# Queueing the preparation of a head pair six steps earlier, with the hi/lo split kept at its place

## The chip, the core and the metric

One core of a Trainium2 chip runs the whole program. The time is the device time of one execution in microseconds (us); the figures shown are medians over several executions. A profile is one execution taken apart by the hardware profiler.

## What is computed

Attention with a cluster mask, then a dense two-layer MLP, then a routed one (8 experts). The part that matters here is the attention, over batch 2, 8 heads, 768 positions and 64 channels:

```python
q_assign = np.argmax(np.einsum('bhsd,hcd->bhsc', q_n, c_n), axis=-1)
k_assign = np.argmax(np.einsum('bhsd,hcd->bhsc', k_n, c_n), axis=-1)
mask = q_assign[:, :, :, None] == k_assign[:, :, None, :]
scores = scale * np.matmul(q, k.transpose(0, 1, 3, 2))
scores = np.where(mask, scores, -1000000000.0)
...
attn = np.exp(scores)
attn = attn / (np.sum(attn, axis=-1, keepdims=True) + 1e-09)
return np.matmul(attn, v).astype(np.float32)
...
h = x @ w_in
g = np.maximum(0.01 * h, h)
return (g @ w_out).astype(np.float32)
```

## The kernel before, in words

The 16 (batch, head) problems are taken as 8 pairs of heads. A pair is 12 steps, so the attention is 96 steps, and it fills about the first 300 us. A step s is one head's block of 128 query rows: four score matmuls into PSUM (L343: `sps<-UA/UB`, then `sps<-VA/VB`), the row maximum on DVE (L346), the exponential on ACT (L361), the transposes of the block of step s-3 (L400) and their evacuation on ACT (L407), and a share of the products with v (L415). Even steps are head 0 of the pair and read the tiles UA and VA, odd steps head 1 and read UB and VB. There are two PSUM buffers for scores, so PE can be one step ahead of ACT's exponential and no more.

**Preparation of a pair.** U and V hold q and k, each as a high and a low part, and in rows 64 to 79 of U the cluster mask. They are double buffered over pairs. They are made in a chain: load q and k (`natq`, `natk`, L99, on SP's queue); four groups of transposes on PE (`raw_pe`, L179, one per half of q and k); four copies to `raw` on ACT (`raw_act`, L186); a split of each into high and low on POOL (`raw_split`, L205 and L206); after the second half of q and of k, four copies each between the halves of U and V on SP's queue (L210 to L218, 64 x 768 float32 each; for k in the order `UB<-UA`, `VA<-VB`, `VB<-UA`, `VA<-UA`); beside it the cluster scores (`assign_pe`, `assign_act`), the argmax on DVE and POOL, the transposes of its result (`mask_pe`) and `mask_dve` (L289 and L294), which scales the mask on DVE and writes it into U by eight small copies on SP's queue, four into UA, then four into UB.

**What sets the order.** The step loop issues everything in program order, and each engine runs its instructions in that order. A table `PREP` says for each part of the chain in which step r it is issued, r counted from the start of the pair ahead (r = 0 of pair 2 is step 12). Before, the chain starts at r = -2 and its mask copies go out at r = 8. Pair 1 has a table of its own (`PREP1`), since its q and k are prepared ahead of the loop; pair 0 is prepared ahead of the loop altogether.

**Other traffic.** Every 5.5 steps `conv_step` stores one converted piece of the MLP's weights (L544, `w_f_scratch<-cvt`, 512 KB) and loads another (L519, `stg`, 1 MB), both on ACT's queue: at steps 10.5, 16, 21.5, 27, 32.5, 38, 43.5, 49, 54.5, 60, 65.5, 71, 76.5 and so on. Every six steps ACT's queue also gets the store of the reciprocals of the row sums (L652, at s = 6n + 3) and two loads that spread them over partitions (L386, `rb`, at s = 6n + 5); POOL then scales the output and splits it (`av_split`, L430 to L432).

**Semaphores of transfers.** In the built program the transfers that SP and ACT issue are given one of eight semaphores (DMAHW0 to DMAHW7) in rotation, and the instruction that issues a transfer first waits until the transfer that had its semaphore before has landed. It stands in its engine's order meanwhile. On ACT such a wait also holds the exponentials behind it, and two score buffers later it holds PE.

Of the kernel before, what the change touches and what calls it, by code (L numbers as in the profile page):

```python
# [20 lines left out]
def _f(ap):  # L21
    return ap.bitcast(F32)
# [3 lines left out]
def kernel(  # L26
# [66 lines left out]
    def load_qk(p):  # L93
        b, cc = divmod(p, NPAIR)
        for nm, src in (("q", q), ("k", k)):
            if p:
                t = att_a.tile([P, NT, 2, D], F32, tag="nat" + nm, name="nat" + nm)
                nat[nm, p] = t
                nc.sync.dma_start(t, src[b, 2 * cc:2 * cc + 2].rearrange("h (p t) d -> p t h d", t=NT))  # L99
            else:  # L100
                t = att.tile([P, 2, HS], F32R, tag="pr", name="first", bufs=4)
                t = _f(t.rearrange("p a b -> p (a b)")).rearrange("p (h t d) -> p h t d", h=2, d=D)
                nc.sync.dma_start(t, src[b, 0:2].rearrange("h (p t) d -> p h t d", t=NT))
                first[nm] = t
                nat[nm, 0] = nat0[:, "qk".index(nm)]
            if p == 0 and nm == "q":
                nc.sync.dma_start(cnat, centroids.rearrange("h c d -> (h c) d"))
# [59 lines left out]
    raw_t, uv_t, sc_t, oh_t = {}, {}, {}, {}  # L167
# [14 lines left out]
    def raw_act(p, i):  # L182
        qk, half = divmod(i, 2)
        ps = ps_prep.pop(("raw", i)).rearrange("p j c -> p (j c)")
        sc = SCALE if qk == 0 else 1.0
        nc.scalar.activation(out=raw_t[p][:, i, :], in_=ps, func=AF.Copy, scale=sc)  # L186
        if p:
            raw_split(p, i)

    def first_hi(i):  # L190
# [7 lines left out]
    def raw_split(p, i):  # L198
        raw = raw_t[p]
        UA, UB, VA, VB = uv_t[p]  # L200
        qk, half = divmod(i, 2)
        cs = slice(half * HS, (half + 1) * HS)
        hi = UA[:, qk, cs]
        lo = (VA if qk == 0 else VB)[:, qk, cs]
        nc.gpsimd.tensor_scalar(out=hi, in0=raw[:, i, :], scalar1=1.0, scalar2=1.0, op0=ALU.mult, op1=ALU.mult)  # L205
        nc.gpsimd.tensor_tensor(out=lo, in0=raw[:, i, :], in1=_f(hi), op=ALU.subtract)  # L206
        if half == 1:
            dma = nc.sync.dma_start
            U, W, X, Y = (_f(t[:, qk, :]) for t in (UA, UB, VA, VB))
            dma(W[0:64], U[64:128])  # L210
            if qk == 0:
                dma(Y[0:64], X[64:128])
                dma(Y[64:128], U[64:128])
                dma(X[64:128], U[0:64])
            else:
                dma(X[64:128], Y[0:64])
                dma(Y[0:64], U[64:128])
                dma(X[0:64], U[0:64])  # L218
# [67 lines left out]
    def mask_dve(p):  # L286
        UA, UB, VA, VB = uv_t[p]
        mk = att_a.tile([P, HS], F32R, tag="mk", name="mk")
        nc.vector.tensor_scalar(out=mk, in0=ps_prep["mk"].rearrange("p j c -> p (j c)"), scalar1=msc[:, 0:1],  # L289
                                scalar2=msc[:, 1:2], op0=ALU.mult, op1=ALU.add)  # L290
        for h, U in ((0, UA), (1, UB)):
            for i in range(4):
                qk, half = divmod(i, 2)
                nc.sync.dma_start(_f(U[64:80, qk, half * HS:(half + 1) * HS]),  # L294
                                  _f(mk[32 * i + 16 * h:32 * i + 16 * h + 16, :]))

    PREP = [
        (-2, "pb", raw_pe, 0), (-1, "a0", raw_act, 0), (-1, "pb", raw_pe, 1),
        (0, "a0", raw_act, 1), (0, "pb", raw_pe, 2), (1, "a0", raw_act, 2), (1, "pb", raw_pe, 3),
        (2, "a0", raw_act, 3), (2, "pb", assign_pe, None),  # L300
        (3, "a0", assign_act, None), (3, "pb", argmax_pe, None),
        (4, "d", argmax_0, None), (4, "d", argmax_1, None), (5, "d", argmax_2, None), (6, "d", argmax_3, None),
        (7, "pb", mask_pe, None), (8, "d", mask_dve, None),
    ]
    PREP1 = [(1, "pb", assign_pe, None), (2, "a0", assign_act, None), (2, "pb", argmax_pe, None), (3, "pb", argmax_0, None), (4, "pb", argmax_1, None), (5, "d", argmax_2, None), (6, "pb", argmax_3, None), (7, "pb", mask_pe, None), (8, "d", mask_dve, None)]

    def prep(p, r, slot):
        if p >= NP:
            return
        for rr, sl, f, arg in PREP1 if p == 1 else PREP:  # L310
            if rr == r and sl == slot:
                if f is raw_pe or f is raw_act:
                    f(p, arg)
                else:
                    f(p)
                if f is raw_act and arg == 3 and 1 < p < NP - 1:
                    load_qk(p + 1)
# [137 lines left out]
    UA, UB, VA, VB = uv_t[0]  # L455
# [27 lines left out]
    for r in range(3, 7):  # L483
        for slot in ("a0", "pa", "d", "pb"):
            prep(0, r, slot)
# [82 lines left out]

    def preps(p, r, slot):
        prep(p + 1, r, slot)  # L570
        if r >= 10:
            prep(p + 2, r - 12, slot)

    CONV0, CPER = 10, 11
# [62 lines left out]
    for s in range(NSTEP + 12 + LAG):  # L637
        p, r = divmod(s, 12)
        if s < NSTEP:
            st_scores(s)  # L640
        conv_step(s, 0)
        preps(p, r, "a0")
        preps(p, r, "pa")
        if 0 <= s - LAG < NSTEP:
            st_transpose(s - LAG)
# [17 lines left out]
        if 0 < gf <= NSTEP // 6 and rf < 2:  # L663
            recip(gf - 1, rf)
        preps(p, r, "d")
        preps(p, r, "pb")
        if r == 10 and p + 1 < NP:
# [703 lines left out]
```

## Time and profile before

| | before |
|---|---|
| runs | 712.04, 716.92, 717.11 us |
| median | 716.92 us |
| the profiled execution | 715.46 us, span 713.8 us |
| mean granted TensorE clock | 0.98 |
| PE busy | 657.3 us, 92% of the span |
| ACT, DVE, POOL busy | 424.6, 397.9, 261.1 us |

In the rows below, a timeline row gives start (us from the start of the span), duration in us, engine, line, operation, what it writes and reads, count, and in brackets how long the engine was idle ahead of it and what is taken to have released it. SPq and ACTq are the instructions with which SP and ACT issue transfers; their duration is that of the issue, not of the transfer.

### The profile page before, as it was taken

To read this page: it belongs to the slowest core of one execution; us is meant where nothing else is said; L and a number is where in the kernel's file an instruction comes from. 1 tells how busy PE (TensorE), PEld (TensorE's weight loads), DVE (VectorE), ACT (ScalarE), POOL (GpSimd) and SP (SyncE) were. 2 spreads that over 40 slices of the span, in tenths; PEclk is the share of its full clock that TensorE was granted. 3 is DMA by queue.
4 is the path that set the end of the run, shared out by engine and by line. 5 is a ranking of instruction groups with operands and counts; after the bars stand their busy time and mean duration, and the time that the engine had idled before them with its cause. 6 is when DMAs were issued, how large, how long until landed. Compare 5 with 4: busy or idle time off the path is not lost. (4 is left out here: it accounts for less than half of the span.)

```text
span 713.8 us, 10056 instructions
## 1 busy us (share of the span) xinstructions
PE 657.3 (92%) x3587; PEld 490.9 (69%) x3587; DVE 397.9 (56%) x687; ACT 424.6 (59%) x824; POOL 261.1 (37%) x263
## 2 busy tenths in 40 slices
PE   5869997989998999989999999999999989989995
PEld 3646664656665656568888888788888767767875
DVE  5747773767785667332222312543223637999993
ACT  5857875778787678644444444445444354757771
POOL 4222422425344211274456444444434356000412
PEclk9989998999999899999999999999999999999998
DMA  8776684666768554820000200003233147989970
GB/s 196 214 207 181 190 206 133 165 196 177 220 177 261 148 166 159 308 98 1 0 1 2 118 2 1 0 1 124 112 118 118 65 172 277 338 287 310 369 253 25
DMA packets 64723, 108.79 MB, mean 152 GB/s; under 512 B 27481, under 2 KB 33083, under 8 KB 63648
## 3 DMA queue, kind: packets, MB, share of 16 engines
q1 hardware_dynamic: 52944, 71.30, 32.8%
q10 hardware_dynamic: 9696, 30.46, 13.1%
q0 software_dynamic: 2032, 6.37, 2.6%
q8 instruction: 29, 0.48, 0.3%
q14 instruction: 22, 0.18, 0.1%
HBM read 77.71 MB, written 16.89 MB: 133 GB/s over the span
## 5 line engine op out<-in xcount | busy, mean ns | idle before, releaser
L346 DVE TENSOR_REDUCE st<-sps 128x1 f32<-128x768 f32 x96 | 91.6, 955 | 85.5 <-PE sps L343 85.0
L704 DVE TENSOR_TENSOR g<-ups,lk 128x512 f32<-128x512 f32 x48 | 33.2, 691 | 136.3 <-ACT lk L703 136.2
L407 ACT ACTIVATE pt<-tps 128x384 f32<-128x384 f32 x192 | 84.3, 495 | 36.0 <-PE tps L400 35.1
L361 ACT ACTIVATE pr<-sps,st 128x768 f32<-128x768 f32 x96 | 86.9, 906 | 22.4 <-DVE cvt L537 5.5
L607 POOL TENSOR_TENSOR wloi<-rawb,whii 128x512 fp32r<-128x512 f32 x36 | 46.6, 1294 | 105.5 <-ACT whii L605 105.5
L415 PE MATMUL avps<-pt,vnat 128*64 128x384 f32 x384 | 83.9, 521 | 0.0
L400 PE MATMUL tps<-ident,pr 128*128 128x128 f32 x576 | 81.4, 278 | 1.6 <-ACT pt L407 1.5
L400 PEld LDWEIGHTS tps<-ident,pr 128*128 128x128 f32 x576 | 69.8, 143 | 9.0 <-ACT pt L407 5.1
L631 PE MATMUL ups<-xh,wloi 128*128 128x512 f32 x192 | 74.8, 390 | 0.9 <-POOL wloi L607 0.9
L631 PE MATMUL ups<-xh,whii 128*128 128x512 f32 x192 | 74.8, 390 | 0.0
L631 PE MATMUL ups<-xl,whii 128*128 128x512 f32 x192 | 74.7, 389 | 0.0
L719 PE MATMUL acc<-wloo,gh 128*128 128x512 f32 x184 | 71.8, 390 | 2.0 <-POOL wloo L617 2.0
L719 PE MATMUL acc<-whio,gh 128*128 128x512 f32 x184 | 73.4, 399 | 0.0
L719 PE MATMUL acc<-whio,gl 128*128 128x512 f32 x184 | 71.8, 390 | 0.0
L703 ACT ACTIVATE lk<-ups 128x512 f32<-128x512 f32 x48 | 28.6, 595 | 65.6 <-PE ups L631 65.6
L430 POOL TENSOR_TENSOR xr<-xr,rb 128x384 f32<-128x384 f32 x16 | 16.4, 1023 | 103.0 <-ACT xr L423 86.5
L705 ACT ACTIVATE gh<-g 128x512 fp32r<-128x512 f32 x48 | 30.4, 632 | 38.3 <-DVE g L704 38.3
L706 DVE TENSOR_TENSOR gl<-g,gh 128x512 fp32r<-128x512 f32 x48 | 34.3, 715 | 33.5 <-ACT gh L705 33.5
L617 POOL TENSOR_TENSOR wloo<-rawb,whio 128x512 fp32r<-128x512 f32 x36 | 46.4, 1290 | 0.9 <-ACT whio L616 0.8
L343 PE MATMUL sps<-UB 80*128 80x384 f32 x96 | 30.6, 398 | 14.6 <-ACT pr L361 6.3
L932 DVE TENSOR_TENSOR xl<-rawb,xh 128x1024 fp32r<-128x1024 f32 x36 | 42.3, 1216 | 0.3 <-ACT xh L930 0.3
L631 PEld LDWEIGHTS ups<-xh,wloi 128*128 128x128 f32 x192 | 36.0, 188 | 8.8 <-POOL wloi L607 1.3
(291 smaller groups left out, 1341.7 us busy)
## 6 DMA issues: line engine op xcount, KB each, us to landing
rawb<-in_moe_w_dram SPq DMA_DIRECT2D x26, 1024.0 KB
stg<-in_moe_w_in_dram ACTq DMA_DIRECT2D x8, 1024.0 KB
w_f_scratch<-cvt ACTq DMA_DIRECT2D x16, 512.0 KB
stg<-in_moe_w_out_dram ACTq DMA_DIRECT2D x8, 1024.0 KB
rawa<-in_moe_w_dram SPq DMA_DIRECT2D x8, 1024.0 KB
rawb<-w_f_scratch SPq DMA_DIRECT2D x6, 1024.0 KB
vnat<-in_v_dram SPq DMA_DIRECT2D x8, 384.0 KB
rb<-recip_scratch ACTq DMA_DIRECT2D x32, 96.0 KB
```

The source lines that it names most:

```text
L346: nc.vector.tensor_reduce(out=st[:, 0:1], in_=ps[:, :, 0:HS], axis=AX.XY, op=ALU.max, negate=True)
L361: nc.scalar.activation(out=pr, in_=ps[:, :, 0:HS], func=AF.Exp, bias=st[:, 0:1], accum_out=sm_t[g][:, 3 * h + j:3 * h + j + 1])
L400: nc.tensor.transpose(ps[:, t, :], pr[:, kh, t * P:(t + 1) * P], ident)
L407: nc.scalar.activation(out=pt[:, 3 * kh:3 * kh + 3, j, :], in_=t_t[s][kh], func=AF.Copy)
L415: nc.tensor.matmul(av_t[g][64 * h:64 * h + 64, :], lhsT=vnat[p][:, h, kt, :], rhs=pt_t[p, half, h][:, kt].rearrange("p j c -> p (j c)"), s ...
L607: eng.tensor_tensor(out=lo, in0=src, in1=_f(hi), op=ALU.subtract)
L617: nc.gpsimd.tensor_tensor(out=lo, in0=src, in1=_f(hi), op=ALU.subtract)
L631: nc.tensor.matmul(ps, lhsT=w[:, cc, :], rhs=x[:, cc, cs], start=(n == 0), stop=(n == 3 * KD - 1))
L704: nc.vector.tensor_tensor(out=g, in0=ps, in1=t, op=ALU.max)
L706: nc.vector.tensor_tensor(out=gl, in0=g, in1=_f(gh), op=ALU.subtract)
L719: nc.tensor.matmul(ps, lhsT=a[:, ts_], rhs=w, start=(fc == 0 and n == 0), stop=(fc == NFC - 1 and n == 2))
L932: eng.tensor_tensor(out=lo, in0=src, in1=_f(hi), op=ALU.subtract)
```

## The change

The table becomes a function `plan(d)`: `PREP = plan(0)` starts the raw transposes at r = -8 and ends the mask on DVE at r = 2, six steps earlier than before. Pair 2 uses `plan(4)` (two steps earlier than before) and pair 3 `plan(2)` (four). `raw_split` no longer follows the raw copy at once: it has entries of its own at r = 0 to 3, one step later than before, and with it go its copies on SP's queue (r = 1 and 3 instead of 0 and 2). The eight mask copies become `mask_dma`, issued at r = 4 (pair 2: r = 6) instead of r = 8. The loads of the next pair's q and k, issued behind the last raw copy, move with it from r = 2 to r = -4. Pair 1 stays as it was. After the change the lines from L294 on stand later (scores L359, exponential L377, `rb` L402, reciprocal store L668, `stg` L535, mask copies L301).

```diff
-        if p:
+        if p == 1:
             raw_split(p, i)
...
+        mk_t[p] = mk
+
+    mk_t = {}
+
+    def mask_dma(p):
+        UA, UB, VA, VB = uv_t[p]
+        mk = mk_t.pop(p)
         for h, U in ((0, UA), (1, UB)):
...
-        (-2, "pb", raw_pe, 0), (-1, "a0", raw_act, 0), (-1, "pb", raw_pe, 1),
...
-        (7, "pb", mask_pe, None), (8, "d", mask_dve, None),
...
+    def plan(d):
+        return [
+            (d - 8, "pb", raw_pe, 0), (d - 7, "a0", raw_act, 0), (d - 7, "pb", raw_pe, 1),
...
+            (d, "d", argmax_3, None), (d + 1, "pb", mask_pe, None), (d + 2, "d", mask_dve, None),
+            (0, "a0", raw_split, 0), (1, "a0", raw_split, 1), (2, "a0", raw_split, 2), (3, "a0", raw_split, 3),
+            (max(d + 2, 4), "d", mask_dma, None),
+        ]
+
+    PREP = plan(0)
...
+    PREPS = {0: PREP0, 1: PREP1, 2: plan(4), 3: plan(2)}
...
-        if r >= 10:
+        if r >= 4:
             prep(p + 2, r - 12, slot)
```

Three places show how instructions move. The first is PE around the end of step 8 and the start of step 9. The names: `rcps` is the transpose of the reciprocals, `rawps` the raw transposes, `natq` pair 2's q. Before:

```order
L343 MATMUL sps<-UA 128x384 [waits Activation_49]
L343 MATMUL sps<-UA 128x384
L343 MATMUL sps<-VA 128x384 x2
L400 MATMUL tps<-ident,pr 128x128 [waits Activation_49]
L400 MATMUL tps<-ident,pr 128x128 x2
L400 MATMUL tps<-ident,pr 128x128 [waits Activation_49]
L400 MATMUL tps<-ident,pr 128x128 x2
L378 MATMUL rcps<-ident,rc_114 128x128 [waits DVE_49,Activation_49]
L343 MATMUL sps<-UB 128x384 x2
```

The same place after the change:

```order
L394 MATMUL rcps<-ident,rc_114 128x128 [waits DVE_49,Activation_49]
L179 MATMUL rawps<-ident,natq 128x128 [waits DMAHW6_49,DVE_49]
L179 MATMUL rawps<-ident,natq 128x128 x2
L359 MATMUL sps<-UB 128x384 x2
L359 MATMUL sps<-VB 128x384 x2
```

Pair 2's first raw transposes moved from step 10 to the end of step 8, and the wait for the load of `natq` (on DMAHW6) now stands ahead of the scores of step 9.

The second is POOL at pair 3's split (steps 23 to 27; L205 writes the high part, L206 the low one). Before:

```order
L432 TENSOR_TENSOR xl<-xr,xh 128x384 [waits Pool_49]
L205 TENSOR_SCALAR UA<-raw 128x384 [waits DMAHW1_49,DMAHW6_49,DMAHW0_49,Activation_49]
L206 TENSOR_TENSOR VA<-raw,UA 128x384 [waits DMAHW2_49,PE_49,Pool_49]
L205 TENSOR_SCALAR UA<-raw 128x384 [waits Activation_49]
L206 TENSOR_TENSOR VA<-raw,UA 128x384 [waits Pool_49]
L205 TENSOR_SCALAR UA<-raw 128x384 [waits Activation_49]
L206 TENSOR_TENSOR VB<-raw,UA 128x384 [waits PE_49,Pool_49]
L205 TENSOR_SCALAR UA<-raw 128x384 [waits Activation_49]
L206 TENSOR_TENSOR VB<-raw,UA 128x384 [waits Pool_49]
L430 TENSOR_TENSOR xr<-xr,rb 128x384 [waits DMAHW2_49,DMAHW1_49,Activation_49]
```

After:

```order
L206 TENSOR_TENSOR VA<-raw,UA 128x384 [waits PE_49,Pool_49]
L251 TENSOR_TENSOR eq<-eq,cw 128x384 [waits DVE_49]
L205 TENSOR_SCALAR UA<-raw 128x384
L206 TENSOR_TENSOR VA<-raw,UA 128x384 [waits Pool_49]
L205 TENSOR_SCALAR UA<-raw 128x384 [waits Activation_49]
L206 TENSOR_TENSOR VB<-raw,UA 128x384 [waits PE_49,Pool_49]
L446 TENSOR_TENSOR xr<-xr,rb 128x384 [waits DMAHW4_49,DMAHW3_49,Activation_49]
L447 TENSOR_SCALAR xh<-xr 128x384 [waits Pool_49]
L448 TENSOR_TENSOR xl<-xr,xh 128x384 [waits Pool_49]
L205 TENSOR_SCALAR UA<-raw 128x384
L206 TENSOR_TENSOR VB<-raw,UA 128x384 [waits Pool_49]
```

The last quarter of the split, whose result SP copies, moved from ahead of `av_split` to behind it.

The third is ACT's queue in steps 27 to 29, and the copies of SP that share semaphores with it. ACT before:

```order
L544 DMA w_f_scratch<-cvt 128x1024 [waits DMAHW0_49,DVE_49]
L519 DMA stg<-in_moe_w_in_dram 128x2x1024 [waits DMAHW2_49]
...
L652 DMA recip_scratch<-rrow 6x128 [waits DMAHW6_49,Activation_49]
...
L386 DMA rb<-recip_scratch 64x384 [waits DMAHW1_49,DMAHW6_49,DMAHW0_49,Pool_49]
L386 DMA rb<-recip_scratch 64x384 [waits DMAHW1_49]
L361 ACTIVATE pr,sm<-sps,st 128x768 [waits DVE_49]
```

ACT after:

```order
L560 DMA w_f_scratch<-cvt 128x1024 [waits DMAHW1_49,DVE_49]
L535 DMA stg<-in_moe_w_in_dram 128x2x1024 [waits DMAHW2_49]
...
L402 DMA rb<-recip_scratch 64x384 [waits DMAHW5_49,DMAHW6_49,DMAHW4_49,DMAHW3_49]
L402 DMA rb<-recip_scratch 64x384 [waits DMAHW7_49]
L377 ACTIVATE pr,sm<-sps,st 128x768 [waits DVE_49]
```

SP after, the copies of the split's k half in step 27 and the first mask copies of step 28:

```order
L210 DMA UB<-UA 64x768 [waits DMAHW3_49,Pool_49]
L216 DMA VA<-VB 64x768 [waits DMAHW4_49,Pool_49]
L217 DMA VB<-UA 64x768 [waits DMAHW5_49,DMAHW4_49]
L218 DMA VA<-UA 64x768 [waits DMAHW7_49]
L301 DMA UA<-mk 16x384 [waits DMAHW0_49,DVE_49]
L301 DMA UA<-mk 16x384 [waits DMAHW1_49]
L301 DMA UA<-mk 16x384 [waits DMAHW5_49,DMAHW3_49,DMAHW2_49]
```

The copies `VB<-UA` and `VA<-UA` of step 27 hold DMAHW5 and DMAHW7, and the two `rb` loads of step 29 are the next to use these; the third mask copy waits for DMAHW5 too. Before, the copies of this pair stood in step 26, and no `rb` load took the semaphore of a copy less than 5.5 steps old. The same pattern stands at steps 75 and 77 (pair 7's copies, DMAHW1 and DMAHW3), with the conversion's transfers of step 76.5 between them.

## Rows read from the trace of the kernel before

**Rows 1.** Windows of the trace, with the columns start:end, length, busy us and count of PE, PEld, DVE, ACT and POOL, the granted clock PEclk, the busy share of the DMA engines and GB/s.

```profile
49.60:56.40 6.80, 4.27 (x15) 2.48 (x15) 1.96 (x4) 1.86 (x4) 0.06 (x1) 0.51 0.58 140
57.00:117.00 60.00, 54.84 (x341) 35.30 (x339) 43.05 (x67) 44.62 (x101) 20.19 (x24) 1.00 0.71 195
118.00:124.60 6.60, 6.36 (x22) 4.65 (x23) 2.69 (x3) 4.56 (x12) 1.82 (x3) 0.50 0.26 76
231.00:237.20 6.20, 6.20 (x21) 4.47 (x22) 1.69 (x4) 2.35 (x5) 1.09 (x2) 0.50 0.61 142
```

**Rows 2.** Timeline of PE, steps 9 to 25: the scores of step 9, pair 2's first raw transposes (step 10) and its third (step 12), the scores of step 13 (two rows), and those of step 25.

```profile
34.81 0.60 PE L343 MATMUL sps<-UB 80*128 80x384 f32 x2
...
39.74 0.52 PE L179 MATMUL rawps<-ident,natq 128*128 128x128 f32 x3 [0.17 <-DMA natq<-in_q_dram]
...
44.00 0.55 PE L179 MATMUL rawps<-ident,natq 128*128 128x128 f32 x3 [1.58 <-ACT raw L186]
...
49.37 0.41 PE L343 MATMUL sps<-UB 80*128 80x384 f32 x1 [2.19 <-DMA rb<-recip_scratch]
...
52.31 0.69 PE L343 MATMUL sps<-UB 80*128 80x384 f32 x1 [2.53 <-DMA UB<-mk]
...
86.04 0.66 PE L343 MATMUL sps<-UB 80*128 80x384 f32 x2
```

**Rows 3.** Timeline of PE, the scores of steps 35, 47, 73 and 85.

```profile
118.24 1.01 PE L343 MATMUL sps<-UB 80*128 80x384 f32 x2 [4.38 <-ACT pr L361]
...
156.76 0.61 PE L343 MATMUL sps<-UB 80*128 80x384 f32 x2 [1.45 <-ACT pr L361]
...
230.97 1.06 PE L343 MATMUL sps<-UB 80*128 80x384 f32 x2 [2.22 <-DMA rb<-recip_scratch]
...
266.59 0.59 PE L343 MATMUL sps<-UB 80*128 80x384 f32 x2 [1.36 <-DMA UB<-mk]
```

**Rows 4.** Timeline of ACT and of the transfers that it issues (ACTq), at steps 33, 43.5, 45, and at the conversion's transfers and the `rb` loads of steps 16 to 77.

```profile
64.19 0.47 ACTq L519 DMA_DIRECT2D stg<-in_moe_w_out_dram  x1
...
77.59 0.34 ACTq L544 DMA_DIRECT2D w_f_scratch<-cvt  x1
...
92.44 2.28 ACTq L519 DMA_DIRECT2D stg<-in_moe_w_in_dram  x1
...
100.29 1.12 ACTq L386 DMA_DIRECT2D rb<-recip_scratch  x2
...
117.20 0.90 ACT L361 ACTIVATE pr<-sps,st 128x768 f32<-128x768 f32 x1 [5.31 <-DMA UA<-mk]
...
129.97 0.46 ACTq L519 DMA_DIRECT2D stg<-in_moe_w_out_dram  x1
...
146.95 0.38 ACTq L519 DMA_DIRECT2D stg<-in_moe_w_in_dram  x1
...
155.38 0.28 ACTq L652 DMA_DIRECT2D recip_scratch<-rrow  x1
155.71 0.90 ACT L361 ACTIVATE pr<-sps,st 128x768 f32<-128x768 f32 x1 [3.44 <-DVE cvt L537]
...
245.54 0.45 ACTq L519 DMA_DIRECT2D stg<-in_moe_w_out_dram  x1
...
247.08 0.45 ACTq L386 DMA_DIRECT2D rb<-recip_scratch  x1
```

**Rows 5.** Timeline of SP's queue: the copies `VA<-VB` and `VB<-UA` of the k half for pairs 3, 4 and 7 (the second waits for the landing of the first), and pair 6's mask copies.

```profile
91.50 0.46 SPq L216 DMA_DIRECT2D VA<-VB  x1
...
95.79 0.46 SPq L217 DMA_DIRECT2D VB<-UA  x1
...
133.24 0.95 SPq L216 DMA_DIRECT2D VA<-VB  x1
...
141.06 0.46 SPq L217 DMA_DIRECT2D VB<-UA  x1
...
218.21 4.54 SPq L294 DMA_DIRECT2D UA<-mk  x4
222.79 2.80 SPq L294 DMA_DIRECT2D UB<-mk  x4
...
238.49 0.46 SPq L216 DMA_DIRECT2D VA<-VB  x1
...
241.23 0.46 SPq L217 DMA_DIRECT2D VB<-UA  x1
```

**Rows 6.** Timeline of POOL: the first operation of `av_split` at steps 15, 27 and 75, its last one at step 27, and one quarter of a split (pair 4).

```profile
60.52 1.01 POOL L430 TENSOR_TENSOR xr<-xr,rb 128x384 f32<-128x384 f32 x1 [1.36 <-ACT xr L423]
...
92.55 1.00 POOL L430 TENSOR_TENSOR xr<-xr,rb 128x384 f32<-128x384 f32 x1 [1.07 <-ACT xr L423]
...
94.23 1.00 POOL L432 TENSOR_TENSOR xl<-xr,xh 128x384 fp32r<-128x384 f32 x1
...
131.61 0.51 POOL L205 TENSOR_SCALAR UA<-raw 128x384 fp32r<-128x384 f32 x1 [2.58 <-ACT raw L186]
132.21 1.01 POOL L206 TENSOR_TENSOR VB<-raw,UA 128x384 fp32r<-128x384 f32 x1
...
240.41 1.01 POOL L430 TENSOR_TENSOR xr<-xr,rb 128x384 f32<-128x384 f32 x1 [1.95 <-ACT xr L423]
```

More of the change, by code (lines that the diff above doesn't have):

```diff
@@ L295, in mask_dve @@
                                   _f(mk[32 * i + 16 * h:32 * i + 16 * h + 16, :]))
-    PREP = [
-        (-2, "pb", raw_pe, 0), (-1, "a0", raw_act, 0), (-1, "pb", raw_pe, 1),
[L299 to L302, printed above, removed]
-        (7, "pb", mask_pe, None), (8, "d", mask_dve, None),
-    ]
-    PREP1 = [(1, "pb", assign_pe, None), (2, "a0", assign_act, None), (2, "pb", argmax_pe, None), (3, "pb", argmax_0, None), (4, "pb", argmax_1, None), (5, "d", argmax_2, None), (6, "pb", argmax_3, None), (7, "pb", mask_pe, None), (8, "d", mask_dve, None)]
+    def plan(d):
+        return [
+            (d - 8, "pb", raw_pe, 0), (d - 7, "a0", raw_act, 0), (d - 7, "pb", raw_pe, 1),
+            (d - 6, "a0", raw_act, 1), (d - 6, "pb", raw_pe, 2), (d - 5, "a0", raw_act, 2), (d - 5, "pb", raw_pe, 3),
+            (d - 4, "a0", raw_act, 3), (d - 4, "pb", assign_pe, None),
+            (d - 3, "a0", assign_act, None), (d - 3, "pb", argmax_pe, None),
+            (d - 2, "d", argmax_0, None), (d - 2, "d", argmax_1, None), (d - 1, "d", argmax_2, None),
+            (d, "d", argmax_3, None), (d + 1, "pb", mask_pe, None), (d + 2, "d", mask_dve, None),
[3 more added lines that the diff above has]
+    PREP = plan(0)
+    PREP0 = [(3, "a0", assign_act, None), (3, "pb", argmax_pe, None), (4, "d", argmax_0, None), (4, "d", argmax_1, None),
+             (5, "d", argmax_2, None), (6, "d", argmax_3, None)]
+    PREP1 = [(1, "pb", assign_pe, None), (2, "a0", assign_act, None), (2, "pb", argmax_pe, None), (3, "pb", argmax_0, None), (4, "pb", argmax_1, None), (5, "d", argmax_2, None), (6, "pb", argmax_3, None), (7, "pb", mask_pe, None), (8, "d", mask_dve, None),
+             (8, "d", mask_dma, None)]
+    PREPS = {0: PREP0, 1: PREP1, 2: plan(4), 3: plan(2)}
     def prep(p, r, slot):
@@ L309, in prep @@
             return
-        for rr, sl, f, arg in PREP1 if p == 1 else PREP:
+        for rr, sl, f, arg in PREPS.get(p, PREP):
             if rr == r and sl == slot:
-                if f is raw_pe or f is raw_act:
+                if arg is not None:
                     f(p, arg)
```

## The prediction

> **What bounds the kernel now.** I read the windows first. From 57 to 117 us PE is busy 54.84 of 60 us at a granted clock of 1.00 [rows 1]: in the attention PE is the bound, and only a stretch in which PE stands idle, or runs at half clock, can be won. The windows show three such stretches: 49.6 to 56.4, 118 to 124.6 and 231 to 237.2, at 0.50 or 0.51, the lower of the clock's two levels (1.2 instead of 2.4 GHz). Each begins behind an idle PE. The price of one is half of PE's busy time in it: 4.27/2 = 2.1, 6.36/2 = 3.2 and 6.20/2 = 3.1 us [rows 1].
>
> The timeline of PE then gives the idle times and what ended them. Step 12 waited 1.58 us for ACT's raw copy, step 13 waited 2.19 and 2.53 us [rows 2]. Step 35 waited 4.38, step 47 1.45, step 73 2.22 and step 85 1.36 us [rows 3]. At two places (49.37 and 230.97) the profile names an `rb` load, which these score matmuls don't read; what they do read and what came last is the mask in UB, so I count both as waits for mask copies. The waits of steps 35 and 47 come from ACT: its exponential at 117.20 started after 5.31 us of idleness, ended by a landing `UA<-mk`, and that at 155.71 after 3.44 us [rows 4]. The second stood behind a store of reciprocals that was issued at 155.38, when the 1 MB load issued at 146.95 had landed, 8.4 us after its issue: the semaphores in rotation. PE lost 0.93 us less than ACT at the first (5.31 to 4.38) and 1.99 less at the second (3.44 to 1.45).
>
> **How long a copy takes.** The change moves 64 x 768 copies against the conversion's loads, so their price decides. `VB<-UA` is issued when `VA<-VB` has landed, so the gap between the two rows is the time of a copy [rows 5]: undisturbed 2.74 us (238.49 to 241.23); issued 0.9 us ahead of the 1 MB load at 92.44, 4.29 us (91.50 to 95.79); issued 3.3 us into the load of 129.97, 7.82 us (133.24 to 141.06). The last landed 141.06 - 129.97 = 11.1 us after the load's issue; the load of 146.95 itself took 8.4. My rule: a copy issued into a load lands 8.4 to 11.1 us after the load's issue.
>
> A rule of the Trainium skill speaks for less: DMA: Bandwidth & Descriptors, section "Anatomy of one DMA — SWDGE (gpsimd) path", fits a transfer's time as about 2.0 us plus its bytes at 436 GB/s. It is for transfers issued by GpSimd, and these are SP's; by it 196,608 bytes would take an estimated 2.45 us, close to the undisturbed row, with nothing for the load beside it, and the sum would come out as rival B's, not mine. The row with 7.82 us contradicts it here.
>
> **The change part by part** (times of before; against 715.46 us, the profiled execution's own time, which lies 1.46 below the median of 716.92).
>
> (a) Pair 2's transposes, steps 8 to 13. They now stand ahead of step 9's scores, which began at 34.81, and need `natq`, which landed at about 39.7: PE waited 0.17 for it there, [rows 2]. Wait: 39.7 - 34.8 = 4.9. Behind the idle times of step 13, 35 and 73 (2.2 us and more) half clock followed, behind those of steps 12, 47 and 85 it did not [rows 1 to 3]; here I count it, 3.2. For that the mask copies of pair 1, which are not behind PE, land during the wait: 2.19 + 2.53 go, the raw copy's 1.58 too, and the half clock of 49.6 (2.1). Sum 4.9 + 3.2 - 6.3 - 2.1 = -0.3.
>
> (b) Pair 2's split, steps 15 to 21. The last quarter of the split stands behind `av_split`, which starts at 60.52 and takes 94.23 + 1.00 - 92.55 = 2.7 us; a quarter takes 132.21 + 1.01 - 131.61 = 1.6 [rows 6]. So `VA<-VB` goes out at 64.9, into the load of 64.19, and lands at 72.6 to 75.3 by my rule, `VB<-UA` 2.7 later. The third mask copy waits for it and the others for the third; the store at 77.59 (step 21.5) and the load behind it use the semaphores of the fourth and fifth mask copy [rows 4]. Landing at about 79 to 82, they hold ACT for 1.2 to 4.1 us, say 2.8; less the 0.93 to 1.99 of above, PE +1.4. From below, nothing, if the copy takes 2.74.
>
> (c) Steps 27 to 35. Before, the split's copies left at 91.50; now behind `av_split` (92.55 + 2.7) and a quarter (1.6), so at 96.9, into the load of 92.44. `VA<-VB` lands at 100.8 to 103.5, `VB<-UA` and the `VA<-UA` issued 0.46 behind it at 104.0 to 106.7. The `rb` loads wait for these two; ACT comes to them at 100.29 [rows 4], or up to 0.8 earlier, since a pair's assign work has left the steps ahead. ACT waits 3.7 to 7.2, I take 6.0; behind it stand the exponentials, so PE waits 5.1. The wait of step 35 goes (the mask copies leave four steps earlier), 4.38. Half clock follows either. Sum +0.7; by the undisturbed copy 2.1 - 4.4 = -2.3.
>
> (d) Step 47: the store behind the load of 146.95 gets another neighbour in the rotation, 0.3 left of 1.45: -1.1.
>
> (e) Step 73: pair 6's mask copies left at 218.21 to 225.59 [rows 5], and leave four steps earlier, some 12 us by (266.59 - 230.97)/12 = 2.97 a step [rows 3]; the last of them still meet the load of step 65.5, but are needed only at 228.8. Wait and half clock go: -2.2 - 3.1 = -5.3.
>
> (f) Steps 75 to 77, pair 7: as (c), but the conversion stands between the copies and the `rb` loads. `av_split` at 240.41, plus 2.7 and 1.6: `VA<-VB` at 244.8, 0.7 ahead of the load at 245.54, so 4.3 us, landed at 249.1. Only then `VB<-UA` goes, into the load: landed 245.54 + 8.4 to 11.1 = 254.0 to 256.6. The `rb` load came at 247.08 [rows 4]. ACT waits 6.9 to 9.5, say 8.5; PE 7.6, and half clock behind it 3.1: +10.7. Before, these copies were out at 241.23 and cost nothing. By the undisturbed copy (247.5, then 250.7 for the last) ACT waits 3.6, PE 2.7.
>
> (g) Step 85's wait, 1.36, goes, since PE comes 7 us later: -1.4. The raw transposes, the assign matmuls and the loads of q and k cost what they did, in other steps: nothing, under PE's 54.84 of 60 us.
>
> Sum: -0.3 + 1.4 + 0.7 - 1.1 - 5.3 + 10.7 - 1.4 = +4.7. 715.5 + 4.7 = 720.2 us.
>
> **The rivals.**
>
> B, faster: copies take 2.74 us also beside a load. For it: two of three rows are under 4.3. Against it: 7.82. Then (b) is 0, (c) -2.3, (f) +2.7: -0.3 + 0 - 2.3 - 1.1 - 5.3 + 2.7 - 1.4 = -7.7, 707.8 us; 711 if the clock falls at step 77, 705 if it stays up at step 29 as well. The page named above sits here.
>
> C, slower: pair 2's mask is late. By (b) its last copies into UB leave at 80 to 83, with the load of step 21.5 right behind. UB is read at step 25, 86.04 plus the 1.4 of (b). It decides from a landing later than 87.4. As copies issued just ahead of a load take 4.3, 83 + 4.3 = 87.3 is the edge. Past it, I price as step 13: 2.5, and half clock 3.1: 725.8 us.
>
> D, slower, the change not doing what it says: the masks leave no earlier in effect, because the third mask copy of a pair waits for the semaphore of its `VB<-UA`. Then (e) and (g) stay unwon: 720.2 + 6.7 = 726.9 us. Against it: pair 6 has four steps of slack.
>
> **How the numbers follow.** My forecast 0.52, B 0.20, C 0.13, D 0.08, and 0.07 for what I don't see. Two executions of this kernel differ by about 1%, so within 1% of the median means 709.8 to 724.1. The forecast's own range, 716 to 725, goes by the ends of (b), (c) and (f) taken partly together; a tenth of the whole chance, 0.11, lies over 724. B is faster in three cases of four. Faster: 0.15 + 0.03 of the unseen = 0.18. Slower: 0.11 + 0.13 + 0.08 + 0.03 = 0.35. Within 1%: 0.41 + 0.05 + 0.01 = 0.47. The range that leaves out two in ten: 705 (B without the clock's fall) to 727 (D).
>
> **What would show it.** In the profile after: PE waits for `natq` near 34.8, about 4.9 us, and none for a mask at step 13; POOL's last quarter of pairs 2, 3 and 7 behind `av_split`; the gap between `VA<-VB` and `VB<-UA` at pairs 2, 3 and 7 (7.8 or 2.7); ACT held at the `rb` loads of steps 29 and 77 for 6.0 and 8.5 us; the half clock at 231 moved to step 78; no wait at steps 35, 73 and 85. Wrong if the copies land in under 3 us beside a load (B), if ACT reaches the `rb` loads later than I place it, or if step 25 waits for UB (C). If the waits at steps 29 and 77 together pass 16.6 us on PE (12.7 here), the kernel is slower by over 1%.

## The result and the profile after

| | before | after |
|---|---|---|
| median of 20 runs | 716.40 us | 724.12 us |
| ratio after / before | | 1.0145 (1.0114 to 1.0177) |
| profiled execution | 715.46 us, span 713.8 | 721.19 us, span 719.5 |
| mean granted clock | 0.980 | 0.974 |

The forecast was 720.2 us, 705 to 727. Ratios here and below leave disturbed runs of either kernel out, so they can differ from the quotient of two medians.

To see where the time went, take from the timeline of PE the start of each step's scores (`sps<-UA` or `sps<-UB`) in both traces and compare the length of stretches. Every difference of a stretch below is worked out that way, from one execution of each kernel, so it also holds what two executions of one program differ by. In the first stretch the two are of different kinds, as the part on the prediction shows.

| stretch | before | after | difference | term of the sum |
|---|---|---|---|---|
| steps 8 to 15 | 32.71 to 63.06 | 33.12 to 59.27 | -4.2 | (a) -0.3 |
| steps 16 to 23 | to 83.32 | to 82.50 | +3.0 | (b) +1.4 |
| steps 24 to 27 | to 96.16 | to 92.61 | -2.7 | |
| steps 28 to 35 | to 123.13 | to 123.49 | +3.9 | (c) +0.7 |
| steps 36 to 43 | to 145.99 | to 146.58 | +0.2 | |
| steps 44 to 47 | to 159.41 | to 161.77 | +1.8 | (d) -1.1 |
| steps 48 to 71 | to 225.87 | to 230.09 | +1.9 | |
| steps 72 to 77 | to 247.63 | to 245.18 | -6.7 | (e) -5.3 |
| steps 78 to 83 | to 262.81 | to 271.18 | +10.8 | (f) +10.7 |
| steps 84 and 85 | to 268.91 | to 275.89 | -1.4 | (g) -1.4 |

Steps 0 to 7 add 0.4, from step 86 to the end of the span it is -1.3, and the whole is 719.5 - 713.8 = +5.7 us.

The longest idle times of PE in the changed kernel, from its timeline, stand against [rows 2, 3]:

```profile
37.31 0.88 PE L179 MATMUL rawps<-ident,natq 128*128 128x128 f32 x3 [1.83 <-DMA natq<-in_q_dram]
...
107.92 0.90 PE L179 MATMUL rawps<-ident,natk 128*128 128x128 f32 x3 [6.77 <-ACT raw L186]
...
132.61 0.33 PE L394 MATMUL rcps<-ident,rc 128*128 128x128 f32 x1 [2.10 <-ACT pt L423]
...
151.03 0.33 PE L394 MATMUL rcps<-ident,rc 128*128 128x128 f32 x1 [2.84 <-ACT pt L423]
...
256.52 1.01 PE L359 MATMUL sps<-UB 80*128 80x384 f32 x2 [8.92 <-ACT pr L377]
```

The wait of 2.10 us belongs to step 38, which took 4.63 us before and 4.76 after. None of the mask waits of steps 13, 73 and 85 is left, nor the wait of step 35. In their place stand two larger ones that end with ACT, at steps 30 and 78. ACT's timeline shows what held it there (against [rows 4], where the `rb` loads at 100.29 and 247.08 went out when ACT reached them):

```profile
105.09 1.35 ACTq L402 DMA_DIRECT2D rb<-recip_scratch  x2
106.49 0.90 ACT L377 ACTIVATE pr<-sps,st 128x768 f32<-128x768 f32 x1 [8.19 <-DMA VA<-UA]
...
148.52 0.43 ACTq L535 DMA_DIRECT2D stg<-in_moe_w_in_dram  x1
149.00 1.22 ACT L546 ACTIVATE cvu<-stg 128x512 f32<-128x512 f32 x2 [1.98 <-DMA UA<-mk]
...
254.04 1.39 ACTq L402 DMA_DIRECT2D rb<-recip_scratch  x2
255.48 0.90 ACT L377 ACTIVATE pr<-sps,st 128x768 f32<-128x768 f32 x1 [9.99 <-DMA VA<-UA]
```

Ahead of each exponential the `rb` loads are issued late, and what ends the idle time is the landing of `VA<-UA`, the last copy of the split. Neither the exponential nor the load reads it; it had the semaphore that the second load takes next. Not all of the hold at step 29 is the copies': the store of the reciprocals, which the `rb` loads do read, was issued at 93.22 beside the conversion's load of 91.00, and by the semaphore increments in the trace it landed at 100.79, 2.5 us after ACT had come to the loads (106.49 - 8.19 = 98.30). From there on the copies held it, `VB<-UA` until 104.94 and `VA<-UA` until 105.70. At step 77 the store had landed at 241.34, before ACT came, and all of the hold is the copies'.

The copies themselves, on SP's queue (pairs 2, 3 and 7; against [rows 5]):

```profile
63.79 0.46 SPq L216 DMA_DIRECT2D VA<-VB  x1
68.87 0.46 SPq L217 DMA_DIRECT2D VB<-UA  x1
...
96.64 0.46 SPq L216 DMA_DIRECT2D VA<-VB  x1
102.21 0.46 SPq L217 DMA_DIRECT2D VB<-UA  x1
...
244.16 0.46 SPq L216 DMA_DIRECT2D VA<-VB  x1
251.25 0.46 SPq L217 DMA_DIRECT2D VB<-UA  x1
```

A copy took 5.1, 5.6 and 7.1 us (the gaps), beside conversion loads issued at 60.19, 91.00 and 242.97. POOL shows why they left so late (against [rows 6]): the quarter of the split that they read (L205, L206) follows the end of `av_split` (L448):

```profile
93.86 1.01 POOL L448 TENSOR_TENSOR xl<-xr,xh 128x384 fp32r<-128x384 f32 x1
94.84 0.69 POOL L205 TENSOR_SCALAR UA<-raw 128x384 fp32r<-128x384 f32 x1
95.61 1.00 POOL L206 TENSOR_TENSOR VB<-raw,UA 128x384 fp32r<-128x384 f32 x1
...
241.24 1.32 POOL L448 TENSOR_TENSOR xl<-xr,xh 128x384 fp32r<-128x384 f32 x1
242.52 0.51 POOL L205 TENSOR_SCALAR UA<-raw 128x384 fp32r<-128x384 f32 x1
243.12 1.01 POOL L206 TENSOR_TENSOR VB<-raw,UA 128x384 fp32r<-128x384 f32 x1
```

The windows behind the waits of steps 8, 30 and 78 show the clock (columns as in [rows 1]): 0.53, 0.70 and 0.53 granted, where these waits were 1.8, 6.8 and 8.9 us.

```profile
36.00:42.00 6.00, 4.69 (x17) 3.27 (x17) 3.04 (x5) 2.69 (x6) 0.00 (x0) 0.53 0.55 126
107.50:114.00 6.50, 6.08 (x30) 4.85 (x30) 3.54 (x7) 4.92 (x12) 0.00 (x0) 0.70 0.36 90
...
256.00:262.00 6.00, 5.48 (x18) 3.86 (x19) 2.46 (x6) 3.98 (x10) 0.00 (x0) 0.53 0.16 43
```

### The profile page after: what moved, and what is told of

The parts are those of the page before. It is cut to its first block, busy times and chain, and to the rows that moved or that the text cites. A ratio compares the mean times of both kernels' runs of the same rounds, so it can differ in the third digit from the quotient of the medians.

```text
span 719.5 us, 10048 instructions
## 1 busy us (share of the span) xinstructions
PE 658.3 (91%) x3587; PEld 494.2 (69%) x3587; DVE 396.2 (55%) x687; ACT 425.1 (59%) x824; POOL 269.1 (37%) x263
## 5 line engine op out<-in xcount | busy, mean ns | idle before, releaser
L377 ACT ACTIVATE pr<-sps,st 128x768 f32<-128x768 f32 x96 | 86.9, 906 | 33.8 <-DMA VA<-UA 18.2
L1138 POOL DMA_INDIRECT out_dram<-y,idx_s x8 | 13.6, 1696 | 76.8 <-DVE y L1136 36.0
```

Source lines behind the costliest of these rows:

```text
L377: nc.scalar.activation(out=pr, in_=ps[:, :, 0:HS], func=AF.Exp, bias=st[:, 0:1], accum_out=sm_t[g][:, 3 * h + j:3 * h + j + 1])
```

## The experiments

Theory 1 is the prediction's: the loss is ACT, held at the `rb` loads of steps 29 and 77 by late copies. Its first rival is that the chain's earlier place costs by itself.

**Undoing the late split, whole and in part.** Two kernels from the changed one: all four splits a step earlier, and only the last quarter.

```diff
-            (0, "a0", raw_split, 0), (1, "a0", raw_split, 1), (2, "a0", raw_split, 2), (3, "a0", raw_split, 3),
+            (-1, "a0", raw_split, 0), (0, "a0", raw_split, 1), (1, "a0", raw_split, 2), (2, "a0", raw_split, 3),
```

> The changed kernel with the four splits one step earlier again (r = -1 to 2), everything else as changed. Theory 1 (the loss is ACT held at the rb loads of steps 29 and 77 by late split copies): the last quarter is ahead of av_split again, VA<-VB leaves before or just at the conversion's load, and the two waits of PE (6.8 and 8.9 us) shrink to under 2 us each; 704 to 712 us, ratio to the kernel before 0.98 to 0.995. Rival (the earlier chain itself costs: its transposes, raw copies and loads meet other work): the time stays at 718 to 727 us.

> The changed kernel with only the last quarter of the split moved, from r = 3 to r = 2, ahead of av_split. Theory 1: at step 77 POOL had 3.5 us idle ahead of av_split, so the copies leave some 5 us earlier, ahead of the conversion's load, and the wait of 8.9 us goes; at step 29 the quarter leaves only 2.7 us earlier, still into the load of step 27, and most of the wait of 6.8 us stays: 709 to 716 us. If av_split alone was to blame, both waits go: 704 to 708. If the earlier chain costs, 718 to 727.

Both came out far slower: 736.17 us, ratio 1.028 (1.022 to 1.034), and 741.60 us, ratio 1.036 (1.029 to 1.042). At step 30 the first behaved as theory 1 says (a step of 3.84 us in place of 9.72) and at step 78 in part (7.55 in place of 11.34), but new waits stand elsewhere. In the second, steps 30 and 78 took 8.44 and 7.40 us, so the wait of step 30, too, stayed for the most part. In both the largest new wait is at step 52 (10.33 and 10.25 us against 2.66). SP's queue and ACT there, in the kernel with all four splits earlier:

```profile
182.60 0.46 SPq L217 DMA_DIRECT2D VB<-UA  x1
```

```profile
185.39 0.28 ACTq L668 DMA_DIRECT2D recip_scratch<-rrow  x1
185.72 0.90 ACT L377 ACTIVATE pr<-sps,st 128x768 f32<-128x768 f32 x1 [9.43 <-DMA VB<-UA]
```

In both programs the store of reciprocals of step 51 takes the semaphore that `VB<-UA` of step 50 had. Moving the copies by one step also moved their place in the rotation, so other ACT transfers came to stand behind fresh copies. So "split earlier, no wait" falls as a theory; that ACT is held by the SP copy that had its semaphore stands, and which transfer is hit goes by the order of all transfers.

**The late split alone.** The kernel before with the split one step later and nothing else moved (in the new code, `plan(6)` for pairs 2 to 7).

> The kernel before with the split alone one step later (r = 0 to 3): chain from r = -2 and mask copies at r = 8 as before. In this program's rotation the rb loads of steps 29 and 77 follow on other transfers (a load of k, and UB<-UA, which leaves ahead of VA<-VB). Theory 1 with the semaphores as the cause: the copies are as late as in the changed kernel, but ACT does not stand behind them, PE keeps the waits of steps 13, 35, 47, 73 and 85: 713 to 720 us. Rival (late copies cost wherever the semaphores fall): 724 to 735 us.

It took 710.25 us (10 runs, 706.3 to 719.5; the kernel before beside it 715.87, 13 runs), under the range of either theory. The copies are late, with gaps of 5.7 and 4.2 us, and the `rb` loads did not wait for them:

```profile
90.58 0.51 SPq L216 DMA_DIRECT2D VA<-VB  x1
96.32 0.46 SPq L217 DMA_DIRECT2D VB<-UA  x1
...
238.04 0.46 SPq L216 DMA_DIRECT2D VA<-VB  x1
242.21 0.46 SPq L217 DMA_DIRECT2D VB<-UA  x1
```

```profile
94.89 1.12 ACTq L402 DMA_DIRECT2D rb<-recip_scratch  x2
...
239.67 0.75 ACTq L402 DMA_DIRECT2D rb<-recip_scratch  x1
240.47 0.63 ACTq L402 DMA_DIRECT2D rb<-recip_scratch  x1
```

Both pairs of loads left before `VB<-UA` was even issued, and steps 30 and 78 took 3.63 and 2.36 us. At these two places the late copies cost PE little, since the loads did not have their semaphores next; the 3.63 us go with the store of the reciprocals, which landed at 94.80, just ahead of the loads that read it. On whether this kernel is faster than the one before, see the end of the part on the prediction.

**The `rb` loads on another queue.** All of them by SP, or only those of steps 29 and 77:

```diff
-            nc.scalar.dma_start(rb[64 * h:64 * h + 64, :], ...)
+            (nc.sync if g in (3, 11) else nc.scalar).dma_start(rb[64 * h:64 * h + 64, :], ...)
```

> The changed kernel with the rb loads issued by SP instead of ACT; copies and their times stay. Theory 1: the copies between U and V are as late as before, but SP waits for them instead of ACT, av_split on POOL gets its rb later, and PE's waits at steps 29 to 31 and 77 to 79 go: 701 to 710 us. If the late copies cost by another way (POOL, or the mask behind them), the time stays at 716 to 727.

> The changed kernel with only the rb loads of steps 29 and 77 issued by SP; all other transfers keep their semaphores from step 35 on. Theory 1 (ACT held at these two places): ACT's idle times of 8.2 and 10.0 us there go, the copies stay as late; some of the first is lost again at step 33, whose store follows on a mask copy of pair 3. 704 to 714 us. Rival (late copies cost by another way, and would show at the next wait): 718 to 727.

All on SP: 723.87 us, ratio 1.014 (1.005 to 1.023). Only the two: 719.80 us, ratio 1.017 (1.013 to 1.021; the kernel before beside it 715.88). In both, step 30 took 2.64 us and step 78 2.44 and 2.36 us (9.72 and 11.34 in the changed kernel), so the two waits are gone with the copies still slow (gaps of 6.4 and 3.8 us with all loads on SP, 7.1 and 7.4 with two). The gain did not stay. With two loads moved, POOL, ACT and SP show where it went:

```profile
260.11 1.26 SPq L402 DMA_DIRECT2D rb<-recip_scratch  x2
```

```profile
268.24 0.99 POOL L446 TENSOR_TENSOR xr<-xr,rb 128x384 f32<-128x384 f32 x1 [23.07 <-DMA rb<-recip_scratch]
```

```profile
269.26 1.11 ACTq L402 DMA_DIRECT2D rb<-recip_scratch  x2
270.42 0.90 ACT L377 ACTIVATE pr<-sps,st 128x768 f32<-128x768 f32 x1 [6.07 <-POOL xh L447]
```

The load of step 77 left behind the mask copies in SP's queue, beside a 1 MB load issued at 260.16, POOL came to it at 268.24, and there is one `rb` buffer, so ACT's load of step 83 waited for POOL: step 84 took 8.11 us. With all loads on SP, most of the gain was lost inside the attention as well. The largest new wait is at step 73, which took 8.90 us against 2.51; PE waits there for the argmax, whose part on POOL stood behind an `av_split` that waited for its `rb`:

```profile
237.65 0.50 PE L283 MATMUL ohps<-identb,oh 128*128 128x128 bf16 x3 [6.21 <-DVE oh L261]
```

The attention ended 4.0 us earlier than in the changed kernel (step 95 at 294.17 against 298.20), and the MLP began worse: PE's first wait there for POOL's `wloo` was 6.62 us against 1.81.

**The reciprocals' rows on POOL's queue**, whose transfers have semaphores of their own, in the changed kernel and in the kernel before (both calls become `nc.gpsimd.dma_start`):

> The changed kernel with the reciprocals' store and the rb loads issued by POOL, which has semaphores of its own for its transfers, so ACT waits only at the conversion's transfers. Theory 1: the waits of steps 30, 45 and 78 go, 700 to 710 us. Rival (the chain's earlier place is the cost): 715 or more.

> The kernel before with the same: reciprocals' store and rb loads issued by POOL. Theory 1: the waits of steps 35 and 47 go, the mask waits of 13, 73 and 85 stay: 703 to 712 us, and the changed chain with this edit is 2 to 8 us faster than this kernel, since it takes the mask waits. Rival (the earlier chain costs by itself): this kernel is the faster of the two.

Changed kernel: 716.90 us, 7.2 less than its median without the edit, ratio 1.003 (0.999 to 1.007). Before: 716.27 us, ratio 1.004 (0.999 to 1.008). Steps 30 and 78 took 2.63 and 2.36 us, and step 95 began at 284.71, 13.5 us earlier than in the changed kernel. The whole span is only 4.3 us shorter. Of the 9.2 us given back, 3.4 went where the attention hands over to the MLP (POOL waits for its own `rb` loads, and PE 4.53 us for POOL, in both kernels), and 4.1 at the end: from the start of POOL's last instruction, the store of the output, the span runs on for 11.0 us against 6.9 (10.5 against 7.0 in the kernel before). My times of 700 to 712 left both out.

The chain was not the faster of the two: the medians lie 0.6 us apart, where 2 to 8 us were forecast. In the kept traces step 95 began at 278.90 in the kernel before with this edit, 5.8 us ahead of the changed one with it, and 6.1 us of that arose between steps 8 and 17 (step 8 took 7.42 us, with the wait for `natq`, against 2.12). That does not show the rival right: the kept execution of the kernel before (710.05 us) is the fastest of its ten, the other lies at its median, and two executions of one program differ by as much in these steps, as the part on the prediction shows.

**The conversion's loads three steps later**, at steps 27 and 76.5, first in the changed kernel:

```diff
             elif r == 11:
                 conv_store(m)
-                if m + 2 < NPC:
+                if m + 2 < NPC and m not in (3, 12):
                     conv_load(m + 2)
-                else:
+                elif m + 2 >= NPC:
                     load_f32(m + 2 - NPC, nc.scalar)
+            elif r == 17 and m in (3, 12):
+                conv_load(m + 2)
```

> The changed kernel with the conversion's 1 MB loads of steps 27 and 76.5 issued three steps later. Theory on the copies (they are slow because of the load beside them): the gap from VA<-VB to VB<-UA at pairs 3 and 7 falls from 5.6 and 7.1 us to 2.7 to 3.4. Rival (they are slow among themselves): it stays over 5. The rotation also shifts by one, the rb loads then follow on older copies, so PE's waits at steps 30 and 78 should go by either: 704 to 714 us.

703.61 us, ratio 0.987 (0.978 to 0.997). SP's copies and ACT's `rb` loads:

```profile
96.84 0.46 SPq L216 DMA_DIRECT2D VA<-VB  x1
99.42 0.46 SPq L217 DMA_DIRECT2D VB<-UA  x1
...
237.04 0.46 SPq L216 DMA_DIRECT2D VA<-VB  x1
240.16 0.46 SPq L217 DMA_DIRECT2D VB<-UA  x1
```

```profile
98.05 1.12 ACTq L402 DMA_DIRECT2D rb<-recip_scratch  x2
...
237.53 0.45 ACTq L402 DMA_DIRECT2D rb<-recip_scratch  x1
```

The gaps are 2.6 and 3.1 us (2.6 and 3.2 in a second trace of this kernel): without a load beside them the copies take what the undisturbed row of [rows 5] said, so the load is what slows them. Steps 30 and 78 took 2.64 and 2.36 us, and step 95 began 17.9 us earlier than in the changed kernel.

**Five transfers out of the rotation, copies left late.** The mask copies of pairs 3 and 7 issued by POOL, nothing else:

```diff
-                nc.sync.dma_start(_f(U[64:80, qk, half * HS:(half + 1) * HS]),
+                (nc.gpsimd if p in (3, 7) else nc.sync).dma_start(_f(U[64:80, qk, half * HS:(half + 1) * HS]),
```

> The changed kernel with the mask copies of pairs 3 and 7 alone issued by POOL. Loads, split and copies between U and V stay where they are, but five transfers fewer stand in the rotation ahead of the rb loads of steps 29 and 77, which now follow on older transfers. Theory 1: the copies are as late as in the changed kernel (gaps of 5 to 7 us), ACT's waits of 8.2 and 10.0 us go all the same: 702 to 711 us. Rival (late copies cost by themselves): 716 or more.

```profile
95.70 0.46 SPq L216 DMA_DIRECT2D VA<-VB  x1
101.62 0.46 SPq L217 DMA_DIRECT2D VB<-UA  x1
...
241.19 0.46 SPq L216 DMA_DIRECT2D VA<-VB  x1
249.07 0.46 SPq L217 DMA_DIRECT2D VB<-UA  x1
```

```profile
241.61 0.45 ACTq L402 DMA_DIRECT2D rb<-recip_scratch  x1
```

```profile
252.28 0.96 POOL L301 DMA_DIRECT2D UA<-mk  x2 [10.01 <-DMA VB<-UA]
```

715.44 us, 8.7 less than the changed kernel's median; ratio 0.999 (0.994 to 1.003). The copies are as slow as ever (gaps 5.9 and 7.9), and at step 77 the load left at 241.61, without a wait: step 78 took 2.35 us. This shows most plainly that the semaphore, not the copy, held ACT. At step 30 it was half won (6.04 us; ACT was still idle for 4.13 us):

```profile
101.88 0.90 ACT L377 ACTIVATE pr<-sps,st 128x768 f32<-128x768 f32 x1 [4.13 <-DMA UB<-UA]
```

The first `rb` load had taken over the semaphore of the last copy of the q half, issued at 92.72 and landed at 100.70, and the store of reciprocals that it reads landed at 100.31; both went beside the conversion's load of 90.08. And POOL now stands 10.01 us behind the copies to issue pair 7's mask, for which step 84 waited (5.07 us): the range was missed by these two.

**What the earlier chain is worth without those waits.** The later loads in the kernel before; in the changed kernel with pair 2's chain at its old place (`plan(6)`, then `plan(4)` and `plan(2)` for pairs 3 and 4); and in the changed kernel once more:

> The kernel before with the conversion's loads of steps 27 and 76.5 three steps later, the edit that took the changed kernel to 703.6 us. If that gain comes from ending ACT's waits behind late copies, which this kernel doesn't have, only step 27's 1 us is won here and the waits of steps 13, 35, 47, 73 and 85 stay: 710 to 717 us, and the changed chain is worth some 10 us with the loads at this place. Rival (the later loads are the gain, whatever the chain): 700 to 706 us here too.

> The changed kernel with the two loads three steps later, and pair 2's chain at its old place (plan(6), pair 3 plan(4), pair 4 plan(2)). The wait for natq at step 8 goes (about 6 us with its half clock), the raw copy's and mask's waits of steps 11 to 13 come back (12.4 us for steps 12 and 13 before against 5.8): 701 to 708 us, near to 703.6. Rival (the natq wait is a plain loss): 696 to 700.

> The changed kernel with the two loads three steps later once more, in more rounds, for its ratio to the kernel before. Open is whether the earlier chain is worth anything when no ACT instruction stands behind late copies: if it is (mask waits of steps 13, 73 and 85 gone), the ratio lies under 0.983, clear of the 0.983 to 0.994 that the later loads gave the kernel before; if it is not, it lies at 0.985 to 0.992.

The kernel before with the later loads: 709.51 us, ratio 0.989 (0.983 to 0.994), a little better than I had said. With pair 2 as before: 706.50 us, ratio 0.985 (0.979 to 0.991). The changed kernel again: 706.87 us, ratio 0.992 (0.988 to 0.995). By these ratios the three can't be told apart, and the last lies in the range set for a chain that is worth nothing. All are about 1% faster than the kernel before and 2 to 3% faster than the changed one, and the later loads are what they share.

## Why the prediction was right, and where it was off

The mechanism was the one that was forecast: ACT held at the `rb` loads of steps 29 and 77, 8.2 and 10.0 us (6.0 and 8.5 forecast), PE 6.8 and 8.9 (5.1 and 7.6). That the semaphore makes these waits, all of the second and most of the first, is shown by the kernel with two masks on POOL and by those with the `rb` loads elsewhere; that they are the loss, by the first of these, which is 8.7 us faster with copies as slow. That the conversion's load makes the copies slow is shown by the gaps of 2.6 and 3.1 us without it. The rule for a copy beside a load held: at pairs 2, 3 and 7 it landed 8.7, 11.2 and 8.3 us after the load's issue, against 8.4 to 11.1 forecast.

That the sum came so near (+4.7 against +5.7 in the profiled executions, +7.7 in the medians) is in part luck, since errors of -3.9, +3.2 and +2.9 us in (a), (c) and (d) partly cancel. Most have one root: the times of the conversion's loads and of ACT were taken from the trace of before as if they stood still, but the loads beside these copies left at 60.19, 91.00 and 242.97, 1.4 to 4.0 us earlier than there. One of the signs was missed: the two waits of PE came to 15.7 us together, under the 16.6 set for a loss of 1%, and the kernel is 1.45% slower. By the terms of the sum:

- (a) was -0.3 and measured -4.2, but between two executions that differ there by more than the chain does; see below the list.
- (b) was +1.4, and the wait did not come. The load of step 16 left 4.0 us earlier than in the trace of before and `VA<-VB` only 1.1 us earlier than forecast (63.79 against 64.9), so the copy met only the last part of the load. `VB<-UA` left at 68.87, 7 us before the store of step 21.5. What steps 16 to 23 lost (+3.0) came back in steps 24 to 27 (-2.7), which I read as pair 3's transposes and cluster scores, moved from the second stretch to the first; this was not tested.
- (c) was +0.7 and measured +3.9. The copy landed at 102.2, inside the forecast 100.8 to 103.5, but ACT came to the loads at about 98.3, not at 99.5 to 100.3, and the first 2.5 us of its hold were the wait for the store of the reciprocals, which the sum had not looked at.
- (d) was -1.1 and measured +1.8. The wait of step 47 went, but the load of step 43.5 took the semaphore of pair 4's third mask copy and stood until 148.52. Of the rotation I had followed what it frees here and not what it binds: the one step where not a size but the reasoning failed.
- (e) and (g) were -5.3 and -1.4, and measured -6.7 and -1.4.
- (f) was +10.7 and measured +10.8, with an error inside: `VA<-VB` was priced at 4.3 us as issued 0.7 us ahead of the load. It was issued 1.2 us behind it and took 7.1, then `VB<-UA` under 2.8. The two errors cancel.
- The stretches without a term (steps 36 to 43 and 48 to 71) lost 2.1 us together; why was not traced.

**Term (a).** `natq` of pair 2 stands in SP's queue behind the last copies of pair 1, and these wait for a `VA<-VB` that goes beside two conversion loads. In the kernel before:

```profile
23.59 0.55 SPq L216 DMA_DIRECT2D VA<-VB  x1
33.43 0.46 SPq L217 DMA_DIRECT2D VB<-UA  x1
...
34.63 0.66 SPq L99 DMA_DIRECT2D natq<-in_q_dram  x1
```

In the changed kernel, and in the kernel before with the later loads:

```profile
33.14 0.66 SPq L99 DMA_DIRECT2D natq<-in_q_dram  x1
```

```profile
33.34 0.66 SPq L99 DMA_DIRECT2D natq<-in_q_dram  x1
```

The built program of the last is, instruction for instruction, that of the kernel before up to step 27, and the four programs with the changed chain in the table are the same up to there. Their traces still fall into two kinds, early ones with `natq` issued by the start of step 8 and late ones with it 1.7 us or more behind:

| kernel, one execution each | `VA<-VB` of pair 1 | `natq` issued, from the start of step 8 | steps 8 to 15 |
|---|---|---|---|
| before | 9.8 us | +1.9 us | 30.35 us |
| before, later loads | 9.0 us | +0.1 us | 22.71 us |
| changed | 9.0 us | 0.0 us | 26.15 us |
| changed, two masks on POOL | 8.7 us | -0.2 us | 24.74 us |
| changed, later loads | 9.9 us | +1.7 us | 26.89 us |
| changed, later loads again | 8.8 us | -1.4 us | 22.44 us |
| changed, two `rb` loads on SP | 9.9 us | +2.1 us | 28.79 us |

So -4.2 sets a late execution of the kernel before against an early one of the changed kernel. Late against late the chain gains 1.6 to 3.5 us here; early against early it loses 2.0 to 3.4 or gains 0.3. The forecast price of the wait for `natq`, 4.9 us, was taken from a late trace: PE waited 1.83 us in the changed kernel's, and 3.77 and 4.68 in the two late ones. The waits of step 13, 2.19 and 2.53 us, from which the forecast counted its gain, belong to the late kind too: with the later loads the kernel before waited 1.06 us there.

Rival B (copies of 2.74 us beside a load) is out for these copies: 5.1, 5.6 and 7.1 us beside a load, 2.6 and 3.1 without. The fit of the Trainium skill (DMA: Bandwidth & Descriptors, "Anatomy of one DMA — SWDGE (gpsimd) path"), by estimate 2.45 us for such a copy, comes near the copies without a load and not those beside one. Rival C did not come: step 25 waited for nothing. Nor did D: the mask waits went.

One sentence ahead of the prediction says too much: that before no `rb` load had the semaphore of a copy less than 5.5 steps old. By the built program it holds for the last two copies of a k half alone. The second `rb` load of step 29 had that of `VA<-VB` of step 26, and `rb` loads of steps 17, 41, 53, 65 and 77, too, had semaphores of copies three to five steps old. No term rests on it.

Open is whether the late split alone, or the later loads alone, make the kernel before faster at all. Both came out about 1% faster, in 10 and 4 runs, but their kept traces are of the early kind (steps 8 to 15 in 22.52 and 22.71 us against 30.35), in steps that the second edit does not touch. Of the 20 runs of the kernel before 19 reach from 707 to 724 us, and how often it is early or late is not on record.

## What to carry to other kernels

When transfers of two engines share semaphores in rotation, a wait at issue is a dependency that no line of the source shows: read from the built program, for each transfer that a busy compute engine issues, which transfer had its semaphore before and how old that one is, and do it again after every edit, since moving one group renumbers all behind it. Where a copy is slow, look at what large transfer is in flight beside it before moving the work that feeds it; here moving two loads took 17 to 21 us off the changed kernel, while the earlier chain had cost 7.7. Before a difference is put down to an edit, compare a stretch that both programs share: here two executions of one program lay 7.6 us apart in eight steps. A wait that is moved to another queue is not gone: the engine that then waits, and the single buffer behind it, may give it back six steps later.

## Not expected

- Moving four splits of a pair by one step changed the time by 12 us (724.12 to 736.17), and by moving one quarter of them by 17.5 (to 741.60), though the data are then ready earlier and not later; the work is the same in all three, only its order differs.
- PE fell to half clock behind an idle of 1.8 us at step 8 (0.53 granted from 36 to 42 us), while before, a wait of 1.58 us at 44.00 left it at 1.00 (granted from 40 to 48 us). With two masks on POOL 1.59 us at step 8 were enough (0.69 from 37.5 to 43 us), so the length of an idle time alone did not tell.
- POOL's transfers lengthened the end of the program: with the reciprocals' rows on POOL's queue the span ran on 11.0 and 10.5 us from the start of POOL's last instruction, and 8.2 us with two masks on it, against 6.9 and 7.0 without; what takes that time was not traced.
